# Four more parts of W1 split in the V passes, Q/K's first weights loaded three groups sooner and split one later

## The chip, the cores and the metric

One Trainium2 chip, and of it one core: the program runs on core 0 alone. The metric is the device time of one execution in microseconds (us). A kernel is run several times, and its time is the median.

## The reference, cut to what matters

The input x has 2048 rows of 1024 numbers. Everything starts from one layer norm and ends in one product of two branches:

```python
xn = _layernorm(x)                      # 2048 x 1024
# branch A: attention, 32 heads of 32
qkv = xn @ wqkv                         # wqkv 1024 x 3072
p = softmax(q @ k.T * 32 ** -0.5)
s = (p @ v) @ wo
# branch B: an MLP with the mish activation, 1024 -> 3584 -> 1024
h = xn @ w1 + b1
g = silu((h * tanh(softplus(h))) @ w2)
return x + s * g
```

All inputs are float32. The kernel gets close to float32 products by writing a number as a high part in the format fp32r and a low part (the rest), and adding three products: high by high, high by low and low by high (`THREE`). "Splitting" a weight below means making these two parts: one copy that rounds (the high part) and one subtraction (the low part).

## The kernel before

The program has four stages, one after the other on TensorE (PE).

**Layer norm and V, first pass.** x is read in 16 tiles of 128 rows. A loop over t from 2 to 17 (line 448 on) does one group of V per turn: `v_group(0, t - 2)`, 24 matmuls of 512 columns with the first half of V's weights, and between them the eight transposes of tile t - 1 (`ln_t`). Around that group the turn also does the norm's small steps for later tiles (`ln_a`, `ln_r`, `ln_b`, `ln_x`), the split of the transposed tile (`ln_c`), the load of a later x tile (`x_load`), the store of the group's result (`evac`), from t = 8 on a store of one quarter of a 512-row block of the normed x to DRAM (`xs`, 1 MB), and near the end the loads of the second half of V's weights (`v_load`) and their splits (`v_split`). V's weights of a half come in four pieces of 256 rows; `v_split(i, j, high, rest)` names the engine of the high part and the one of the low part.

**V, second pass.** A loop over t from 0 to 15 with one `v_group(1, t)` per turn and its store `vs`.

**Q and K.** For f from 0 to 15, four groups each (`qk_group`), with the weights of f split by `qk_split(f)` on ScalarE and VectorE. Beside them run jobs (`presplit`) that load half a part of W1 or W2, split it on GpSimd and store it: the parts of W1 that were not split before, then all of W2. From f = 12 on the first head's scores are mixed in (line 558).

**Attention, MLP and the output product**, in an order that a planner (`Plan`) makes from costs written in the program.

What matters around the change is `w1_early`. W1 has 28 parts of 128 columns; the first `W1_V` of them are split during the V passes. Call number f does three things: it stores the finished part f - 2 (`w1s`, 1 MB), loads the raw part f (`w1e`, 0.5 MB in rows of 512 bytes), and lets GpSimd split part f - 1. Its finished parts live in tiles of the tag `w1`, of which there are two, used in turn:

```python
    def w1_tile(name):
        return w1p.tile([P, 2, KT, P], F32R, tag="w1", name=name, bufs=2)
```

`qk_split` takes its tile for Q/K's weights from the same two. So the first Q/K weights, `qkw0`, go into the tile of the last but one part, and their split on ScalarE waits until that part's store has landed in DRAM. The raw parts, the x tiles and V's raw weights share six buffers of the tag `x`.

All loads and stores named here are issued by one engine, SyncE (SP), strictly in the order of the program: an issue that waits for a buffer or for a finished part holds up all that stand behind it. The engines also work in order, each in its own. ScalarE copies each V group's result out of PSUM (`vst`, three buffers) and then makes the high part of the Q/K weights.

In the profile, line 275 is `move` (a DMA between a tile and DRAM of either direction), line 279 is `low` (all low parts, whatever the engine), line 271 is `copy` and line 268 is `act`.

Of the kernel before, what the change touches and what calls it, by code (L numbers as in the profile page):

```python
# [21 lines left out]
NT = S // P  # L22
# [1 line left out]
SCALE = DH ** -0.5  # L24
EPS = 1e-5

W1_V = 16
NS = H * NT
HK = KT // 2

# [183 lines left out]
def body(ctx: ExitStack, tc: tile.TileContext, x, wqkv, wo, w1, b1, w2, out):  # L214
    nc = tc.nc
# [51 lines left out]
    def act(out_, in_, fn, bias=None, scale=1.0):  # L267
        nc.scalar.activation(out_, in_, fn, bias=zero if bias is None else bias, scale=scale)  # L268

    def copy(out_, in_, scale=1.0):  # L270
        nc.scalar.activation(out_, in_, AF.Copy, scale=scale)  # L271

    def move(out_, in_, eng=None):

        (eng or nc.sync).dma_start(out_.bitcast(F32), in_.bitcast(F32))

    def low(eng, out_, in_, high):

        eng.tensor_tensor(out_, in_, high.bitcast(F32), ALU.subtract)  # L279
# [24 lines left out]
    def v_load(i, j):  # L304

        vraw[i, j] = raw = vp.tile([P, 2, 512], F32, tag="x", name=f"vraw{i}_{j}", bufs=XB)
        nc.sync.dma_start(raw, wqkv[j * 256:(j + 1) * 256, 2 * D + i * 512:2 * D + (i + 1) * 512]
                          .rearrange("(k p) f -> p k f", p=P))

    def v_split(i, j, high, rest):  # L310
        raw = vraw.pop((i, j))
        vw[i, j] = w = vp.tile([P, 2, 2, 512], F32R, tag="w", name=f"vw{i}_{j}", bufs=5)
        for k in range(2):
            if high is nc.scalar:
                copy(w[:, 0, k], raw[:, k])
            else:
                high.tensor_copy(w[:, 0, k], raw[:, k])
            low(rest, w[:, 1, k], raw[:, k], w[:, 0, k])

    def v_group(i, t, cut=0, between=None):  # L320
        st = vp.tile([P, 16, DH], F32, tag="vst", name=f"vst{i}_{t}", bufs=3)
        ps = ps1.tile([P, 512], F32, tag="ps", name=f"v{i}_{t}")
        n = 0
        for k in range(KT):
            for a, b in THREE:
                if n == cut and between:
                    between()
                nc.tensor.matmul(ps, xc[t // 4][k // HK][:, a, k % HK, (t % 4) * P:(t % 4 + 1) * P],  # L328
                                 vw[i, k // 2][:, b, k % 2], start=n == 0, stop=n == 3 * KT - 1)
                n += 1  # L330

        def evac():
            copy(st, ps.rearrange("p (h d) -> p h d", d=DH))
            nc.sync.dma_start(vs[i][:, t], st)

        return evac

    def x_load(t):
        xt = vp.tile([P, D], F32, tag="x", name=f"x{t}", bufs=XB)
        nc.sync.dma_start(xt, x[t * P:(t + 1) * P, :])  # L340
        return xt
# [10 lines left out]
    def ln_a(t):  # L352
        xt = xts[t]
        st = vp.tile([P, 2, 6], F32, tag="st", name=f"st{t}", bufs=4)
        mv = vp.tile([P, 2], F32, tag="mv", name=f"mv{t}", bufs=5)
        var = vp.tile([P, 1], F32, tag="var", name=f"var{t}", bufs=5)
        rs = vp.tile([P, 1], F32, tag="rs", name=f"rs{t}", bufs=5)
        for g in range(2):
            nc.vector.bn_stats(st[:, g], xt[:, g * 512:(g + 1) * 512])
        nc.vector.bn_aggr(mv, st)  # L360
        nc.vector.tensor_scalar(var, mv[:, 1:2], EPS, None, op0=ALU.add)
        stat[t] = mv, var, rs

    def ln_r(t):
        mv, var, rs = stat[t]
        act(rs, var, AF.Ln)
        act(rs, rs, AF.Exp, scale=-0.5)

    def ln_b(t):
        mv, var, rs = stat.pop(t)  # L370
        tmps[t] = tmp = vp.tile([P, 1], F32, tag="tmp", name=f"tmp{t}", bufs=3)
        nc.vector.scalar_tensor_tensor(tmp, rs, var, rs, op0=ALU.mult, op1=ALU.mult)
        nc.vector.tensor_scalar(tmp, tmp, -0.5, 1.5, op0=ALU.mult, op1=ALU.add)
        nc.vector.tensor_tensor(rs, rs, tmp, ALU.mult)
        nc.vector.scalar_tensor_tensor(tmp, mv[:, 0:1], -1.0, rs, op0=ALU.mult, op1=ALU.mult)
        tmps[t] = tmp, rs

    def ln_x(t, both=False):
        tmp, rs = tmps.pop(t)
        r = slice(0, D // 2 if both else D)  # L380
        act(xts[t][:, r], xts[t][:, r], AF.Identity, bias=tmp, scale=rs)
        if both:
            r = slice(D // 2, D)
            nc.vector.tensor_scalar(xts[t][:, r], xts[t][:, r], rs, tmp, op0=ALU.mult, op1=ALU.add)

    def ln_t(t):
        xt = xts.pop(t)
        for g in range(2):
            pts_[t, g] = pt = ps1.tile([P, 512], F32, tag="ps", name=f"pt{t}_{g}")
            for k in range(4):  # L390
                nc.tensor.transpose(pt[:, k * P:(k + 1) * P], xt[:, (4 * g + k) * P:(4 * g + k + 1) * P], ident)

    def ln_c(t):
        c, r = t // 4, slice(t % 4 * P, t % 4 * P + P)
        for g in range(2):
            p4 = pts_.pop((t, g)).rearrange("p (k n) -> p k n", k=4)
            copy(xc[c][g][:, 0, :, r], p4)
            low(nc.vector, xc[c][g][:, 1, :, r], p4, xc[c][g][:, 0, :, r])
# [12 lines left out]

    early_w1, w1_steps = {}, iter(range(W1_V + 2))

    def w1_early():
        f = next(w1_steps, None)
        if f is None:
            return
        if f > 1:
            move(w1s[f - 2], early_w1.pop(f - 2)[1])
        if f < W1_V:  # L420
            raw = vp.tile([P, KT, P], F32, tag="x", name=f"w1e{f}", bufs=XB)
            nc.sync.dma_start(raw, w1[:, f * P:(f + 1) * P].rearrange("(k p) f -> p k f", p=P))
            early_w1[f] = [raw, None]
        if 0 < f <= W1_V:
            raw, _ = early_w1[f - 1]
            early_w1[f - 1][1] = w = w1_tile(f"w1p{f - 1}")
            split_w(w, raw, True)
# [12 lines left out]
    v_split(0, 2, nc.scalar, nc.vector)  # L440
    ln_r(1)
    ln_b(1)
    v_split(0, 3, nc.scalar, nc.gpsimd)
    ln_x(1, True)
    ln_a(2)
    ln_r(2)
    xts[3] = x_load(3)
    for t in range(2, NT + 2):
        if t < NT:
            ln_b(t)  # L450
        evac = v_group(0, t - 2, 18 if t == 2 else 8, (lambda: ln_t(t - 1)) if t <= NT else None)
        if t <= NT:
            ln_c(t - 1)
        if t < NT:
            ln_x(t)
        for m in (4, 5, 6) if t == 2 else (t + 4,):
            if m < NT:
                xts[m] = x_load(m)
        if t == 2:
            ln_a(3)  # L460
        if t + 2 < NT:
            ln_a(t + 2)
        if t + 1 < NT:
            ln_r(t + 1)
        if t in (NT - 4, NT - 3):
            for j in range(2):
                v_load(1, 2 * (t - NT + 4) + j)
        if t == NT - 2:
            v_split(1, 0, nc.scalar, nc.vector)
        if t == NT + 1:  # L470
            for j in range(1, 4):
                v_split(1, j, nc.scalar, nc.vector)
        evac()
        if t > 7:
            c, k = t // 4 - 1, t % 4 * 2
            move(xs[c][:, :, k:k + 2], xc[c][k // HK][:, :, k % HK:k % HK + 2])
        if t > NT - 3:
            w1_early()
    for k in (4, 6):
        move(xs[NC - 1][:, :, k:k + 2], xc[NC - 1][1][:, :, k % HK:k % HK + 2])  # L480
# [3 lines left out]
    def qk_load(f):  # L484
        raws[f] = raw_tile(f"qkraw{f}", wqkv[:, (f % 2) * D + f // 2 * P:(f % 2) * D + (f // 2 + 1) * P])
# [7 lines left out]
    for t in range(NT):  # L493
        v_group(1, t)()
        w1_early()
        if t == 9:
            qk_load(0)
        if t == 12:
            qk_split(0)
            qk_load(1)  # L500
    va.close()
# [91 lines left out]
    def load_w1(n):  # L593
# [4 lines left out]
    sp = pool(qb, "sp", 2, side="right")  # L598
    jobs = iter([(1, f, half) for f in range(W1_V, FT) for half in range(2)] +
                [(2, f, half) for f in range(FT) for half in range(2)])  # L600
# [38 lines left out]
    for f in range(2 * KT):  # L639
        for c in range(NC):  # L640
            qk_group(f, c if f < 2 * KT - 1 else (c + 1) % NC)
            presplit()
            if f % 2 and f < 14 and c < 3:
                presplit()
            if c == 0 and f + 1 < 2 * KT:
                qk_split(f + 1)
                if f + 2 < 2 * KT:
                    qk_load(f + 2)
            if f == 8 and c == 0:
                load_head(0)  # L650
            if f == 14 and c == 0:
                load_head(1)
            if f >= 12:
                for kc in range(4):
                    s_mm(0, 4 * (f - 12) + c, kc)
            if f == 2 * KT - 1 and c == 1:
                load_w1(0)
            later.tick()
# [572 lines left out]
    for c in range(NC):  # L1231
        for s in range(4):
            t = 4 * c + s
# [49 lines left out]
```

## Time and profile before

| what | value |
|---|---|
| time, median of 3 runs (lowest to highest) | 3427.58 us (3426.43 to 3434.65) |
| the profiled execution's own time | 3423.3 us |
| its span, first to last instruction | 3421.1 us |
| TensorE busy, share of the span | 3389.4 us, 99% |
| GpSimd busy | 2453.3 us, 72% |
| VectorE busy | 2340.5 us, 68% |
| ScalarE busy | 1942.2 us, 57% |
| mean DMA rate over the span | 155 GB/s |

The table is one execution. The profiled execution is 4.3 us under the median, and 2.2 us of its time lie outside the span. TensorE is busy nearly all the time, so an edit shows in the time only where it changes how long TensorE waits or how fast its clock runs. The other engines' shares are averages over stages that differ much: the DMA engines move 155 GB/s on the whole, but over 300 GB/s in the stages that the change touches.

### The profile page before, as it was taken

Reading aid. Unit: us, or ns where it says so; the run is one execution under the profiler, and the core shown is the slowest. Engines: PE = TensorE matmul, PEld = TensorE weight load, DVE = VectorE, ACT = ScalarE, POOL = GpSimd, SP = SyncE. Lnnn points to the kernel's source line nnn. Section 1 sums busy time; section 2 is a strip of 40 time slices with the busy share of each in tenths; the row PEclk is TensorE's granted clock in tenths of the full one; section 3 lists DMA queues with packets and bytes.
Section 4 is the critical chain, followed back from the end, with each engine's and each line's share of the span. In section 5 each row is a group of like instructions: output and inputs, shape, how many; then the busy total and the mean of one; then the engine's idle time right before and its main releaser. Section 6 shows DMA issues by size and latency. Waiting matters only on the chain.

```text
span 3421.1 us, 45658 instructions
## 1 busy us (share of the span) xinstructions
PE 3389.4 (99%) x17059; PEld 2492.7 (73%) x17059; DVE 2340.5 (68%) x3763; ACT 1942.2 (57%) x3086; POOL 2453.3 (72%) x752
## 2 busy tenths in 40 slices
PE   8999999999999999999999999999999999999999
PEld 7878877677777767777677777777777767777687
DVE  6211226877878777788878787878878788776533
ACT  5211112766666667666666676666666666666621
POOL 0444443988888888888888888888888888888700
PEclk9999999999999999999999999999999999999999
DMA  5989888433334354343434443333445443333482
GB/s 200 326 292 317 301 309 289 124 109 102 118 106 124 102 170 132 116 112 111 124 99 124 149 148 111 112 113 110 124 112 183 123 123 112 112 114 121 136 297 85
DMA packets 289184, 529.60 MB, mean 155 GB/s; under 512 B 88426, under 2 KB 134506, under 8 KB 265706
## 3 DMA queue, kind: packets, MB, share of 16 engines
q1 hardware_dynamic: 269108, 484.74, 46.0%
q10 hardware_dynamic: 19856, 41.95, 3.3%
q8 instruction: 135, 2.21, 0.3%
q14 instruction: 85, 0.70, 0.1%
HBM read 386.89 MB, written 138.67 MB: 154 GB/s over the span
## 4 chain that ended last, share of the span: by engine, by line
PE 87%; DMA 7%; POOL 3%; DVE 2%; SPq 1%; ACT 0%; issue 0%; POOLq 0%; ACTq 0%; DVEq 0%
PE y L1027 18%; PE h L938 17%; PE t L790 13%; PE pv L837 13%; PE s L707 13%; PE op L1124 5%; DMA w2s<-pw 3%; PE v L328 3%; PE qk L631 3%; DMA w1s<-pw 2%; POOL pw L279 1%; DMA w1e<-in_B_w_dram 1%; PE zp L863 1%; DVE mx L713 1%; POOL pw L619 1%; POOL w1p L279 0%
## 5 line engine op out<-in xcount | busy, mean ns | idle before, releaser
L819 POOL TENSOR_TENSOR z<-z,p 128x2048 f32<-128x2048 f32 x448 | 2066.5, 4613 | 192.1 <-ACT p L268 162.5
L268 ACT ACTIVATE p<-t,zero 128x512 f32<-128x512 f32 x2048 | 1384.4, 690 | 636.1 <-PE t L790 618.3
L713 DVE TENSOR_REDUCE mx<-s 128x1 f32<-128x512 f32 x1984 | 1329.6, 686 | 435.4 <-PE s L707 427.8
L1027 PE MATMUL y<-w,act 128*128 128x512 f32 x2688 | 937.4, 391 | 0.6 <-DVE yacc L1047 0.5
L790 PE MATMUL t<-qstack,kstack 128*128 128x512 f32 x2048 | 801.5, 393 | 0.3 <-ACT p L268 0.2
L707 PE MATMUL s<-kstack,qstack 128*128 128x512 f32 x1984 | 779.6, 394 | 3.9 <-DVE mx L713 3.4
L938 PE MATMUL h<-xr,w 128*128 128x512 f32 x2016 | 713.5, 391 | 2.1 <-DMA w<-w1s 2.1
L1027 PEld LDWEIGHTS y<-w,act 128*128 128x128 f32 x2688 | 502.9, 188 | 118.4 <-issue 8.4
L790 PEld LDWEIGHTS t<-qstack,kstack 128*128 128x128 f32 x2048 | 384.0, 188 | 109.0 <-issue 16.8
L707 PEld LDWEIGHTS s<-kstack,qstack 128*128 128x128 f32 x1984 | 371.3, 188 | 126.5 <-issue 24.3
L837 PE MATMUL pv<-p,v 128*32 128x512 f32 x4096 | 459.4, 594 | 0.0
L938 PEld LDWEIGHTS h<-xr,w 128*128 128x128 f32 x2016 | 377.7, 188 | 85.1 <-issue 5.0
L631 PE MATMUL qk<-xc,qkw 128*128 128x512 f32 x1536 | 352.6, 390 | 6.1 <-ACT qkw L271 6.0
L631 PEld LDWEIGHTS qk<-xc,qkw 128*128 128x128 f32 x1536 | 288.9, 188 | 67.3 <-ACT qkw L271 6.4
L837 PEld LDWEIGHTS pv<-p,v 128*32 128x32 f32 x4096 | 123.3, 110 | 282.7 <-issue 282.0
L819 POOL TENSOR_TENSOR z<-p,p 128x2048 f32<-128x2048 f32 x32 | 147.9, 4623 | 243.3 <-ACT p L268 162.3
L1047 DVE TENSOR_TENSOR yacc<-yacc,y 128x512 f32<-128x512 f32 x416 | 283.0, 680 | 52.2 <-PE y L1027 51.4
L938 PE MATMUL h<-xc,w 128*128 128x512 f32 x672 | 242.3, 391 | 0.1
L279 DVE TENSOR_TENSOR qst<-qk,qst 128x512 fp32r<-128x512 f32 x64 | 44.2, 691 | 253.6 <-ACT qst L271 253.6
L271 ACT ACTIVATE qst<-qk 128x512 fp32r<-128x512 f32 x64 | 38.3, 598 | 308.6 <-PE qk L631 235.5
L619 POOL CAST pw<-praw 128x512 fp32r<-128x512 f32 x80 | 50.9, 637 | 195.7 <-DMA w2s<-pw 125.2
L328 PE MATMUL v<-vw,xc 128*128 128x512 f32 x768 | 181.1, 395 | 0.2 <-DVE xc L279 0.2
(93 smaller groups left out, 2366.5 us busy)
## 6 DMA issues: line engine op xcount, KB each, us to landing
w<-w1s SPq DMA_DIRECT2D x112, 1024.0 KB
w<-w2s SPq DMA_DIRECT2D x224, 512.0 KB
w2s<-pw SPq DMA_DIRECT2D x56, 512.0 KB
qstack<-qs SPq DMA_DIRECT2D x96, 256.0 KB
kstack<-ks SPq DMA_DIRECT2D x96, 256.0 KB
praw<-in_B_w_dram SPq DMA_DIRECT2D x80, 256.0 KB
x<-in_A_x_dram SPq DMA_DIRECT2D x32, 512.0 KB
w1s<-w1p SPq DMA_DIRECT2D x16, 1024.0 KB
```

Source lines behind the costliest of these rows:

```text
L268: nc.scalar.activation(out_, in_, fn, bias=zero if bias is None else bias, scale=scale)
L328: nc.tensor.matmul(ps, xc[t // 4][k // HK][:, a, k % HK, (t % 4) * P:(t % 4 + 1) * P], vw[i, k // 2][:, b, k % 2], start=n == 0, stop=n == ...
L631: nc.tensor.matmul(ps, w[:, a, k], xc[c][k // HK][:, b, k % HK], start=n == 0, stop=n == 3 * KT - 1)
L707: nc.tensor.matmul(sp_, qst[h % 3][:, qt * P:(qt + 1) * P], kst[h % 3][:, kc * 512:(kc + 1) * 512], start=True, stop=True)
L713: nc.vector.reduce_max(tiles["mx"][:, qt, kc:kc + 1], tiles[qt, kc], axis=AX.X)
L790: nc.tensor.matmul(tp, kst[h % 3][:, kt * P:(kt + 1) * P], qst[h % 3][:, c * 512:(c + 1) * 512], start=True, stop=True)
L819: nc.gpsimd.tensor_tensor(zs[h], pts[T - 1] if kt == 1 else zs[h], pts[T], ALU.add)
L837: nc.tensor.matmul(pv[h][c * DH:(c + 1) * DH, :], vt[h][:, k, :], pts[T - kt + k][:, c * 512:(c + 1) * 512], start=k == 0, stop=k == NT - 1)
L938: nc.tensor.matmul(t["h"], w1t[n][:, a, k], xts_[c][k // HK][:, b, k % HK], start=i == 0, stop=i == 3 * KT - 1)
L1027: nc.tensor.matmul(t["y"], acts[n][:, p, s * P:(s + 1) * P], w2t[m_][:, q], start=j == 0 and i == 0, stop=j == YB - 1 and i == 2)
L1047: nc.vector.tensor_tensor(ya, ya, t["y"], ALU.add)
L1124: nc.tensor.matmul(ps[t, dh], ohl[t // 4, k][:, a, s * P:(s + 1) * P], wt[k][:, b, r], start=k == 0 and i == 0, stop=k == KT - 1 and i == 2)
```

## The change

There are four edits, all in the V passes and at the start of Q/K.

1. `W1_V` is 20 instead of 16, and `w1_early` is called from t = 10 of the first pass on instead of from t = 14. Each call f therefore comes four groups sooner than before, and there are four calls more; the last one (it stores the last part) is in turn 13 of the second pass in both kernels. The jobs of Q/K lose parts 16 to 19 of W1, which is eight jobs of 80, and the number of slots for jobs falls from 85 to 78.
2. x tiles are loaded three turns ahead instead of four.
3. `qk_load(0)` is issued in turn 6 of the second pass instead of turn 9, and `qk_split(0)` stands in turn 13 instead of turn 12. As part numbers moved too, `qkw0` now takes the tile of part 18; before it took the tile of part 14.
4. The fourth piece of V's first weights gets its low part from VectorE instead of GpSimd, and its split stands behind the norm of tile 1 instead of ahead of it.

```diff
-W1_V = 16
+W1_V = 20
...
-    v_split(0, 3, nc.scalar, nc.gpsimd)
     ln_x(1, True)
+    v_split(0, 3, nc.scalar, nc.vector)
     ln_a(2)
     ln_r(2)
     xts[3] = x_load(3)
...
-        for m in (4, 5, 6) if t == 2 else (t + 4,):
+        for m in (4, 5) if t == 2 else (t + 3,):
             if m < NT:
                 xts[m] = x_load(m)
...
-        if t > NT - 3:
+        if t > NT - 7:
             w1_early()
...
     for t in range(NT):
         v_group(1, t)()
         w1_early()
-        if t == 9:
+        if t == 6:
             qk_load(0)
-        if t == 12:
+        if t == 13:
             qk_split(0)
             qk_load(1)
...
             qk_group(f, c if f < 2 * KT - 1 else (c + 1) % NC)
             presplit()
-            if f % 2 and f < 14 and c < 3:
+            if f % 2 and f < 14 and c in (0, 2):
                 presplit()
```

## The prediction

> **What bounds the kernel now.** I read the page first, for which engine sets the time.
>
> ```profile
> PE 3389.4 (99%) x17059; PEld 2492.7 (73%) x17059; DVE 2340.5 (68%) x3763; ACT 1942.2 (57%) x3086; POOL 2453.3 (72%) x752
> ```
>
> TensorE is busy in 3389.4 of 3421.1 us, so at most 31.7 us can be won by filling its gaps, and any edit costs or gains what it adds to or takes from them. The second view is the list of waits, TensorE's alone:
>
> ```profile
> core 0 of [0], span 3421.1 us
> engine line waited for: us in total, times, longest us
> PE pt L391 <- ACT x L268: 11.9, 2, 9.4
> PE qk L631 <- ACT qkw L271: 6.0, 1, 6.0
> PE s L707 <- DVE mx L713: 3.4, 5, 1.9
> PE h L938 <- DMA w<-w1s: 2.1, 1, 2.1
> PE s L558 <- DVE mx L562: 1.5, 1, 1.5
> ```
>
> Five entries hold 24.9 us. The change touches three: the norm's start (pt), Q/K's first weights (qk), and the first scores (L558), which lie in Q/K. I went to the second one with the timeline from 176 to 236 us, because it is the place that edits 1 and 3 move:
>
> ```profile
> 188.21 1.73 SPq L288 DMA_DIRECT2D qkraw<-in_A_wqkv_dram  x1
> ...
> 204.93 1.26 POOL L279 TENSOR_TENSOR w1p<-w1e,w1p 128x512 fp32r<-128x512 f32 x1
> 206.22 0.32 SPq L275 DMA_DIRECT2D w1s<-w1p  x1
> ...
> 210.11 1.15 ACT L271 ACTIVATE qkw<-qkraw 128x512 fp32r<-128x512 f32 x2 [19.73 <-DMA w1s<-w1p]
> 210.78 1.29 DVE L279 TENSOR_TENSOR qkw<-qkraw,qkw 128x512 fp32r<-128x512 f32 x2 [89.56 <-ACT qkw L271]
> ...
> 210.80 25.42 PE L631 MATMUL qk<-xc,qkw 128*128 128x512 f32 x105 [5.95 <-ACT qkw L271]
> ```
>
> The first Q/K matmul comes at 210.80, after 5.95 us in which TensorE had nothing to do: V's last one ended at 204.85. The raw Q/K weights were issued at 188.21 and are not what is late: ScalarE's copy at 210.11 was released by the landing of a store, w1s from w1p. This is the tile wait: `qkw0` takes the tile of part 14, and that tile is free when part 14 is stored. The chain back is: GpSimd ends part 14's split at 204.93 + 1.26 = 206.19, SP issues the store at 206.22, and it lands just ahead of 210.11. So what ends last at this point is the stream of W1's parts through DMA and GpSimd. The windows say what limits that stream:
>
> ```profile
> core 0: us, PE busy (x) PEld busy (x) DVE busy (x) ACT busy (x) POOL busy (x), PEclk, DMA share, GB/s
> 76.00:102.00 26.00, 26.00 (x136) 21.95 (x135) 13.52 (x38) 14.23 (x27) 0.00 (x0) 1.00 0.85 290
> 94.00:100.30 6.30, 6.30 (x34) 5.29 (x33) 2.70 (x5) 4.32 (x8) 0.00 (x0) 1.00 0.54 161
> 102.00:137.00 35.00, 35.00 (x162) 29.09 (x161) 9.30 (x10) 10.31 (x17) 16.25 (x16) 1.00 1.01 339
> 125.00:135.00 10.00, 10.00 (x46) 8.29 (x45) 0.00 (x0) 1.20 (x2) 6.04 (x7) 1.00 1.05 394
> 137.00:206.50 69.50, 67.84 (x300) 55.84 (x298) 0.00 (x0) 5.99 (x10) 41.14 (x44) 1.00 1.00 329
> 205.00:211.00 6.00, 0.20 (x1) 0.21 (x2) 0.23 (x1) 0.89 (x2) 4.99 (x6) 0.65 0.50 198
> 211.00:213.00 2.00, 2.00 (x5) 1.57 (x6) 1.51 (x3) 1.72 (x4) 1.69 (x1) 0.50 0.00 0
> 213.00:215.00 2.00, 2.00 (x9) 1.55 (x9) 1.51 (x2) 0.00 (x0) 0.00 (x0) 0.84 0.69 161
> ```
>
> Before the clock column stand the engines' busy times; the last three columns are the granted clock, the share of the 16 DMA engines that is busy, and GB/s. From 102 to 206.5 us the DMA engines are busy all the time (1.01 and 1.00), at 339 and then 329 GB/s. TensorE is full up to 204.85, and the DMA is full as well: two bounds run side by side there, and the DMA one finishes later.
>
> **The change part by part.**
>
> *Edits 1 and 3, the parts of W1 and Q/K's first weights.* The sizes, in the answer on DMAs for 150 to 180 us:
>
> ```profile
> w1s<-w1p SPq DMA_DIRECT2D x5, 1024.0 KB
> w1e<-in_B_w_dram SPq DMA_DIRECT2D x5, 512.0 KB
> ```
>
> Before, `qkw0` waits for the store of part 14, ahead of which stand 15 stores and 16 loads of parts. After, it takes the tile of part 18: 19 stores and 20 loads stand ahead. V's stores ahead of it are the same in both, those up to turn 12. So 4 x (1024 + 512) KB = 6.29 MB are added to what must have passed SP's queue before the first Q/K weight can be split. At the 329 GB/s of the long window that is 19.1 us.
>
> What comes in return is an earlier start: the first call moves from about 102 to about 76 us. But the DMA isn't idle there. In 76 to 102 its share is 0.85, so 0.15 x 26 = 3.9 us are free. The four parts thus need 19.1 us, and 3.9 us are there: the store of the last part that matters lands 19.1 - 3.9 = 15.2 us later. Loading Q/K's raw weights three turns sooner doesn't help, as they weren't late, and they only move ahead of three V stores in the same queue. Splitting one turn later than before cancels nothing either: that call of `w1_early` stores part 19, behind the store that `qkw0` waits for. So the gap before Q/K grows from 5.95 to about 21.2 us. **Cost: +15.2 us.** Low end: the four parts at the best rate of the table, 394 GB/s, 16.0 - 3.9 = 12.1. High end: the free 3.9 can't be used, 19.1. I take the middle value, since it rests on the long window in which this very stream runs.
>
> Behind that wait on ScalarE stand the evacuations of V's last two groups; they only feed stores, and who waits for them is PSUM banks, of which there are eight. On SP, part 19's store and the next raw Q/K weights stand behind; the second Q/K weights are needed four groups after the first, and move with them. The clock: during a gap of 5.95 us it falls to 0.50 in the row from 211 and is at 0.84 in the one after. That loss is 2 x 0.50 + 2 x 0.16 = 1.3 us, it is in the time of before, and a longer gap pays it once as well. **0 us.**
>
> *Edit 4 and the start.* The rows of before, from the timeline of the first 32 us (start, time, engine, line):
>
> ```profile
> 16.11 1.14 ACT L271 ACTIVATE vw<-vraw 128x512 fp32r<-128x512 f32 x2
> 16.68 0.21 DVE L372 SCALAR_TENSOR_TENSOR tmp<-rs,var 128x1 f32<-128x1 f32 x1
> 16.80 2.50 POOL L279 TENSOR_TENSOR vw<-vraw,vw 128x512 fp32r<-128x512 f32 x2 [7.19 <-ACT vw L271]
> 16.93 0.15 DVE L373 TENSOR_SCALAR tmp<-tmp 128x1 f32<-128x1 f32 x1
> 17.12 0.99 DVE L374 TENSOR_TENSOR rs<-rs,tmp 128x1 f32<-128x1 f32 x1
> 18.14 1.18 DVE L375 SCALAR_TENSOR_TENSOR tmp<-mv,rs 128x1 f32<-128x1 f32 x1
> 19.36 0.81 ACT L268 ACTIVATE x<-x,tmp,rs 128x512 f32<-128x512 f32 x1 [2.11 <-DVE tmp L375]
> 19.36 0.55 DVE L384 TENSOR_SCALAR x<-x,rs,tmp 128x512 f32<-128x512 f32 x1
> 19.82 1.28 DVE L359 BATCH_NORM_STATS2 st<-x 128x6 f32<-128x512 f32 x2
> ...
> 22.66 0.16 DVE L374 TENSOR_TENSOR rs<-rs,tmp 128x1 f32<-128x1 f32 x1
> ```
>
> GpSimd's two subtractions from 16.80 to 19.30 stand beside two tiny VectorE steps that take 0.99 and 1.18 us, where the same step takes 0.16 at 22.66. So about 1.85 us are lost ahead of tile 1's norm at 19.36. With the subtractions gone from GpSimd, that norm starts at about 17.5. Then ScalarE needs 0.81 for it and 1.14 for the high parts of the fourth piece, to 19.5, and VectorE, which does the two low parts (1.29 a pair of this shape in the row at 210.78), is through at about 20.2 instead of free at 19.82 for the statistics of tile 2. The copies of tile 1 into xc stand behind a step on ScalarE that needs those statistics (`ln_r(2)` ahead of `ln_c(1)`), and TensorE needs them next. They come some 0.35 us later, not sooner: what was won goes to the new work in front. The Trainium skill, "SBUF — State Buffer", section "Who interferes with whom", says that a VectorE instruction with two SBUF inputs and a GpSimd instruction that reads SBUF block each other for the whole instruction; the rows 17.12 and 18.14 agree. By that rule alone edit 4 would gain the 1.85, and the moved parts of edit 1, whose GpSimd work now stands beside the norm's small steps in turns 11 to 17, would pay some of it back; I give both nothing in the sum, for the reason that follows.
>
> TensorE's part of the V passes then ends 0.35 us later, but it has 21 us to wait for the weights. So this is covered. **0 us** (-1.85 to +0.35 if the cover were gone).
>
> *Edit 2*, x one turn later. A tile is then issued one turn ahead of its statistics instead of two. A late one would hold VectorE, and through it TensorE in a later turn; the list of waits of before has no wait of TensorE that a load of x ended, and the same 21 us cover what comes of it. **0 us.**
>
> *Eight jobs fewer in Q/K.* Here TensorE is the bound, and the jobs lie beside it:
>
> ```profile
> 300.00:480.00 180.00, 180.00 (x796) 149.05 (x795) 35.21 (x49) 27.80 (x49) 81.59 (x85) 1.00 0.91 310
> ```
>
> It is busy 180 of 180 us with the DMA share at 0.91. Eight jobs of 256 KB in and 512 KB out take load off, but there is nothing to win where TensorE has no gap. The only gap is the 1.5 us at the first scores (L558 above), which depends on when VectorE gets through the weights of f = 13. It may shrink: 0 to -1.5, I take **-1.0 us**.
>
> **Sum.** 15.2 + 0 + 0 + 0 - 1.0 = +14.2 us. On the profiled execution's 3423.3 us that is 3437.5. The median before, 3427.58, is 4.3 above that execution; the forecast for the median is 3427.58 + 14.2 = 3441.8, rounded **3442 us**, or +0.41%.
>
> **The rivals.**
>
> *The queue speeds up and the gap closes (not slower).* The rate isn't fixed: between 125 and 135 us it was 394 GB/s, with a deep queue. With four parts more in flight from 76 us on, the queue is deep all along. The bytes: 339 x 35 + 329 x 69.5 = 34.7 MB passed from 102 to 206.5; with the four parts 41.0. At 394 the stretch from 76 takes in 26 x (394 - 290) = 2.7 MB beforehand, and 38.3 MB need 97.2 us instead of 104.5. Q/K's weights would be ready before 204.85; the 5.95 and the 1.3 of the clock would go: -7.3 - 1.0 = -8.3, 3419.3 us. It decides from 372 GB/s on, where (41.0 - 26 x 0.082) / 0.372 = 104.5. Against it: in 137 to 206.5 the share is 1.00 at 329 GB/s, so the packets themselves take this time, and the mix (a third of a part's bytes comes in 512-byte rows) stays. Chance 0.10. The Trainium skill, "DMA: Bandwidth & Descriptors", section "Where 436 GB/s comes from", names about 358 GB/s as the limit between HBM and SBUF for a core; held to it, the stream would still be (41.0 - 1.8) / 0.358 - 104.5 = 5 us late. The 394 of the 10 us row lies above that limit, so the measurement stands and the chance stays.
>
> *It speeds up by half.* At 355 GB/s: (41.0 - 1.7) / 0.355 = 110.7, that is +6.2, and +5.2 with the jobs: 3432.8 us. The same rows speak for and against. Chance 0.15.
>
> *SP gets stuck sooner, and a hole opens (worse).* In the changed program's order the last raw piece of V's second weights takes the buffer of the first, so its issue waits until VectorE has split that one in turn 14. Behind it on SP stand a V store, a quarter of xs, part 1's store and part 3's load. Before, such a wait stood at the same place, and the share fell to 0.54 in 94 to 100.3. If the free 3.9 us are not filled and the hole of 6.3 x 0.46 = 2.9 us comes on top: 19.1 + 2.9 - 1.0 = +21.0, 3448.6 us. For it: part 1's store can't leave sooner than that. Against it: enough is queued ahead by then. Chance 0.10.
>
> **How the numbers follow.** The forecast has 0.65. About 0.3%, 10.3 us, is what a measurement of this kernel can tell from no change. Of the forecast's own range, 12.1 - 1.5 = +10.6 to 19.1 - 0 = +19.1, nearly all is above that: 0.60 of its 0.65 slower, 0.05 within. The half case is 0.12 within and 0.03 slower, the worse case 0.10 slower, the closed gap 0.06 within and 0.04 faster. Together slower 0.73, same 0.23, faster 0.04. The range: the half case's middle is +5.2 and the worse case's +21.0; from 3431 (a little under the half case) to 3450 (a little over the worse one) leaves out the closed gap and some tails.
>
> **What would show it.** Right: TensorE's wait for qkw at line 631 at 18 to 24 us, still released by the landing of a w1s store; the DMA share near 1 from 80 us to the start of Q/K; the first Q/K matmul near 226; from there on the same distances as before. Wrong: that wait gone or under 6 us, with V passes moving over 370 GB/s; or TensorE waiting inside the V passes, which would mean x or V's weights came late; or a Q/K stage whose length differs by more than 2 us, which I call bound by TensorE.

## The result, and the profile after

| | before | after |
|---|---|---|
| time, median (lowest to highest), taken in turn on one chip | 3429.43 us (3423.57 to 3434.65), 7 runs | 3440.01 us (3435.78 to 3440.98), 7 runs |
| the profiled execution: time, span | 3423.3, 3421.1 | 3435.78, 3433.9 |

The ratio is 1.0027, with a 95% interval of 1.0015 to 1.0038: the changed kernel is slower by 10.6 us in the medians and by 12.8 us between the two profiled spans. The forecast was +14.2 us, 3442 us; 3440.01 lies in the range.

The page's first row, busy time by engine:

```profile
PE 3391.2 (99%) x17059; PEld 2493.8 (73%) x17059; DVE 2344.3 (68%) x3765; ACT 1943.4 (57%) x3086; POOL 2449.5 (71%) x750
```

TensorE is busy 1.8 us longer in a span that is 12.8 longer: the loss is idle time. The first row of TensorE's list of waits in the changed kernel (columns: engine, tile and line that wait, what ended the wait, then us in total, times, longest):

```profile
PE qk L631 <- ACT qkw L271: 18.7, 1, 18.7
```

The wait for Q/K's first weights has gone from 6.0 to 18.7, inside the 18 to 24 that were forecast. The two waits at L558 (1.5 in the list before, and another of 0.4 below what was quoted) are gone from the list. The timeline of the changed kernel around that wait (start, length, engine and line):

```profile
195.88 0.32 SPq L275 DMA_DIRECT2D w1s<-w1p  x1
...
217.78 1.26 POOL L279 TENSOR_TENSOR w1p<-w1e,w1p 128x512 fp32r<-128x512 f32 x1
219.06 0.32 SPq L275 DMA_DIRECT2D w1s<-w1p  x1
224.43 1.15 ACT L271 ACTIVATE qkw<-qkraw 128x512 fp32r<-128x512 f32 x2 [12.86 <-DMA w1s<-w1p]
225.11 2.50 PE L631 MATMUL qk<-xc,qkw 128*128 128x512 f32 x5 [18.65 <-ACT qkw L271]
```

The store at 219.06 is part 18's (part 19's, the last of 20, follows at 225.18), and with three more stores left out between them the one at 195.88 is part 14's. The chain is the one told before, four parts further on: GpSimd ends part 18's split at 219.04, SP issues its store at 219.06, it lands, ScalarE copies at 224.43, TensorE starts at 225.11. The windows (the last three numbers of a row are the granted clock, the DMA share and GB/s):

```profile
76.00:102.00 26.00, 26.00 (x132) 21.87 (x131) 14.13 (x37) 14.73 (x27) 7.52 (x8) 1.00 0.98 339
102.00:137.00 35.00, 35.00 (x164) 29.12 (x163) 8.24 (x13) 9.77 (x16) 15.80 (x16) 1.00 1.05 396
137.00:206.50 69.50, 69.46 (x307) 57.19 (x305) 0.00 (x0) 6.59 (x11) 39.90 (x43) 1.00 0.97 317
206.50:225.00 18.50, 0.00 (x0) 0.00 (x0) 0.00 (x0) 1.17 (x3) 12.18 (x14) 0.62 0.96 322
```

The DMA engines are full from 76 us to Q/K, as forecast. What was not forecast is the rate in 102 to 137: 396 GB/s against 339 before.

Part of this is one small transfer that changed its place. The load of `b1` (line 481, 14 KB) brings 3584 single numbers of 4 bytes, and it stands on SP behind the last stores of xs. Before, it ran from 134 to 137 us, a stretch with 3584 packets under 512 bytes; in the changed kernel it ran from 146.5 to 150. These stretches as windows, in the kernel before and then in the changed one:

```profile
134.00:137.00 3.00, 3.00 (x15) 2.49 (x14) 0.00 (x0) 0.60 (x1) 0.57 (x1) 1.00 0.92 100
```

```profile
146.50:150.00 3.50, 3.50 (x17) 2.92 (x16) 0.00 (x0) 0.00 (x0) 2.36 (x3) 1.00 0.73 74
```

The DMA engines are busy there for most of the time and move 100 and 74 GB/s. Without the load of b1 the stretch from 102 us on has 361 GB/s before and 396 after, and the one up to 206.5 has 330 in both (after: (317 x 69.5 - 74 x 3.5) / 66 = 330). So 22 of the 57 GB/s by which the first of them became faster, and the whole fall of the second from 329 to 317, are b1's load, which went from the one window into the other.

The whole difference, cut at three events of the two profiled executions (end of V's last matmul; first matmul at L631; the pair of matmuls at L535 that closes the Q/K stage). That last event in the timeline of the kernel before, and then of the changed one:

```profile
578.67 0.33 PE L535 MATMUL mtp<-ident_r,hl 128*128 128x128 f32 x2
```

```profile
589.48 0.33 PE L535 MATMUL mtp<-ident_r,hl 128*128 128x128 f32 x2
```

| stretch | before | after | after - before |
|---|---|---|---|
| start to V's end | 204.85 | 206.46 | +1.61 |
| wait for Q/K's first weights | 5.95 | 18.65 | +12.70 |
| Q/K stage | 367.87 | 364.37 | -3.50 |
| all after it | 2842.43 | 2844.42 | +1.99 |
| span | 3421.1 | 3433.9 | +12.8 |

The first two rows go together: the weights come when the queue brings them, so the first Q/K matmul is 14.31 us later whatever V's end does. The last row is no effect of the change: over all kernels run here this stretch takes 2842.4 to 2844.4, with 20 parts as with 16. That leaves +14.3 - 3.5 = +10.8, which is what the medians show (+10.6).

### The profile page after: what moved, and what is told of

Read it like the earlier page. It is cut to its first block, busy times and chain, and to the rows that moved or that the text cites. A ratio compares the mean times of both kernels' runs of the same rounds, so it can differ in the third digit from the quotient of the medians.

```text
span 3433.9 us, 45655 instructions
## 1 busy us (share of the span) xinstructions
PE 3391.2 (99%) x17059; PEld 2493.8 (73%) x17059; DVE 2344.3 (68%) x3765; ACT 1943.4 (57%) x3086; POOL 2449.5 (71%) x750
## 4 chain that ended last, share of the span: by engine, by line
PE 95%; DVE 2%; DMA 2%; POOL 1%; SPq 1%; ACT 1%; issue 0%; ACTq 0%; POOLq 0%; DVEq 0%
PE y L1027 18%; PE h L938 17%; PE t L790 13%; PE s L707 13%; PE pv L837 13%; PE qk L631 10%; PE op L1124 5%; PE v L328 3%; DMA w1e<-in_B_w_dram 1%; PE zp L863 1%; DVE mx L713 1%; POOL w1p L279 0%; PE pt L391 0%; PE s L558 0%; SPq L275 0%; SPq L334 0%
## 5 line engine op out<-in xcount | busy, mean ns | idle before, releaser
L631 PE MATMUL qk<-xc,qkw 128*128 128x512 f32 x1536 | 352.4, 390 | 18.7 <-ACT qkw L271 18.7
L631 PEld LDWEIGHTS qk<-xc,qkw 128*128 128x128 f32 x1536 | 289.2, 188 | 79.3 <-ACT qkw L271 19.1
```

The lines of the kernel that those rows point to most:

```text
L631: nc.tensor.matmul(ps, w[:, a, k], xc[c][k // HK][:, b, k % HK], start=n == 0, stop=n == 3 * KT - 1)
```

## The experiments

### The number of parts: 16 and 18 with the earlier start

**e1**: the changed kernel with 16 parts, and with them the places for jobs of before.

```diff
-W1_V = 20
+W1_V = 16
-            if f % 2 and f < 14 and c in (0, 2):
+            if f % 2 and f < 14 and c < 3:
```

> The changed kernel with only the number of early parts put back (16, and the slots for the jobs with it); the earlier start, the x loads, the places of the Q/K load and split and the fourth piece stay changed. Queue theory (the bytes ahead of the tile that Q/K's first weights take, at the rate of the DMA): four parts of 1536 KB at 329 GB/s are 19.1 us fewer, so the first Q/K matmul comes at 225.1 - 19.1 = 206.0 at the earliest, that is right after V's last one (206.5): a wait of 0 to 1 us in place of 18.65, no fall of the clock, and 18 to 20 us less than the changed kernel, about 3421 on the median, 7 to 9 under the kernel before. Rival (the place of the split, one turn later, or the load, is what made it late): the wait stays above 10 us.

**e2**: 18 parts, nothing else changed.

> The changed kernel with 18 early parts instead of 20 (76 jobs in 78 slots). Queue theory: two parts fewer ahead, 2 x 1573 KB at 329 GB/s = 9.6 us, first Q/K matmul at 215.5, wait 9.1 us, and 9 to 10 us less than the changed kernel. Loop theory (a part costs a turn of the loop load, split, store, at 5.6 us whatever the bytes): 2 x 5.6 = 11.2, first matmul at 213.9, wait 7.4. Rival (the place of the split): 18 us.

The experiments ran on three chips, so a kernel is compared by its ratio to the kernel before on its own chip. The kernel before took 3429.43 us beside the changed kernel, 3426.01 beside e1 to e4, 3425.78 beside e5 to e8, and 3425.61 (one run) beside e9 to e11.

| parts | first Q/K matmul | wait | time (runs) | ratio to before, 95% |
|---|---|---|---|---|
| 16 (e1) | 207.80 | 2.68 | 3420.08 (11) | 0.9986, 0.9977 to 0.9995 |
| 18 (e2) | 212.19 | 7.00 | 3424.00 (10) | 0.9997, 0.9988 to 1.0006 |
| 20 (changed kernel) | 225.11 | 18.65 | 3440.01 (7) | 1.0027, 1.0015 to 1.0038 |

So the number of parts makes the loss: with 16 the earlier start is a gain. From 18 to 20 parts the first matmul moves by 12.9 us, 6.5 a part. In e2 it came sooner than either theory had it (215.5 and 213.9). These are single executions, and they differ: in e7 below, whose V passes are those of the changed kernel, the first Q/K matmul comes at 223.37 instead of 225.11. By the ratios e1 is 0.41% or 14 us faster than the changed kernel, where 18 to 20 were expected, and its forecast of no wait failed by 2.7 us. The timeline of e1 shows why:

```profile
201.96 0.32 SPq L275 DMA_DIRECT2D w1s<-w1p  x1
202.38 5.20 SPq L334 DMA_DIRECT2D vs<-vst  x4
206.63 0.60 ACT L271 ACTIVATE vst<-v 128x512 f32<-128x512 f32 x1 [4.35 <-DMA vs<-vst]
207.12 1.14 ACT L271 ACTIVATE qkw<-qkraw 128x512 fp32r<-128x512 f32 x2
207.80 10.54 PE L631 MATMUL qk<-xc,qkw 128*128 128x512 f32 x44 [2.68 <-ACT qkw L271]
```

The copy at 207.12 is not released by a store of W1. It starts when ScalarE is done with the evacuation of a V group at 206.63, and that one waited 4.35 us for its buffer, whose store of V stands on SP behind part 15's store at 201.96. Here it is the order on ScalarE that ends last.

### The order on ScalarE, tested: Q/K's first split one turn sooner

**e6** is e1 with the split moved back to where it stood before.

```diff
-        if t == 13:
+        if t == 12:
             qk_split(0)
```

> 16 parts and the 85 places for jobs again, as in e1, and Q/K's first split one turn sooner (t == 12). In e1 2.7 us of waiting were left although the store of part 14 had landed some 7 us earlier; ScalarE's copy stood behind the evacuation of V's group 13, which waited for its buffer. If that order on ScalarE is the whole of the 2.7 us, the wait for qkw at L631 goes, the first Q/K matmul comes at 205.1 to 205.6 and the time is 2.7 us (and up to 1 us of clock) under e1's: 3416 to 3418. The rival: the store still ends last (with part 15 not yet split at t == 12), the evacuation of group 12 then waits on ScalarE for it and 1 to 3 us of wait remain at the banks of V or at qkw: 3419 to 3421.

The same stretch of the timeline in e6:

```profile
202.22 1.14 ACT L271 ACTIVATE qkw<-qkraw 128x512 fp32r<-128x512 f32 x2
...
204.93 13.31 PE L631 MATMUL qk<-xc,qkw 128*128 128x512 f32 x58
```

The weights are split from 202.22 on, and Q/K follows V with no gap. 3418.3 us (11 runs, 3413.18 to 3421.33), ratio 0.998 (0.9971 to 0.9989): 1.6 us more gained on the kernel before than in e1 (7.5 against 5.9), where 2.7 were expected. The clock's part is seen here too: from the first Q/K matmul to the first score at L558 it takes 266.56 us in e6 (471.49 - 204.93), 268.02 in the kernel before (478.82 - 210.80) and 268.12 in the changed kernel (493.23 - 225.11). So its gap costs the kernel before 1.5 us of granted clock (the prediction had 1.3), and the changed kernel's, three times as long, 1.6. Over the other kernels with a gap of 4.5 us or more it is 2.1 to 3.0, with a granted clock of 0.50 in the first 4 to 6 us behind the gap; behind the gaps of 2.7 and 3.1 us in e1 and e9 the clock stays at 1.00 and the difference is 0.4.

### What the earlier start is worth by itself

**e10**: 20 parts as in the changed kernel, but the first call where it was before; the four calls left out come as second calls in four turns of the second pass.

```diff
-        if t > NT - 7:
+        if t > NT - 3:
             w1_early()
...
         w1_early()
+        if t in (1, 4, 7, 10):
+            w1_early()
```

> The changed kernel with 20 parts, but the first part started where the kernel before starts it (t > NT - 3); the four calls that this leaves out come as second calls in turns 1, 4, 7 and 10 of V's second pass. It measures the earlier start by itself. By the prediction's term the earlier start is worth 3.9 us (the free share of the DMA engines between 76 and 102 us): first Q/K matmul near 229. By the stores of part 14 (issued at 206.22 before, at 195.88 in the changed kernel) it is worth 10.3 us: 234 to 236. If doubled calls keep the queue deeper and make the loop faster, it lies under 229.

The timeline of e10 ahead of Q/K, and then its windows:

```profile
205.53 0.32 SPq L275 DMA_DIRECT2D w1s<-w1p  x1
...
233.11 1.15 ACT L271 ACTIVATE qkw<-qkraw 128x512 fp32r<-128x512 f32 x2 [18.67 <-DMA w1s<-w1p]
233.79 2.50 PE L633 MATMUL qk<-xc,qkw 128*128 128x512 f32 x5 [27.57 <-ACT qkw L271]
```

```profile
76.00:102.00 26.00, 26.00 (x132) 21.86 (x131) 13.28 (x37) 14.49 (x27) 0.00 (x0) 1.00 0.84 291
102.00:137.00 35.00, 35.00 (x164) 29.14 (x163) 9.53 (x12) 10.35 (x17) 16.26 (x16) 1.00 1.03 356
137.00:206.50 69.50, 69.22 (x306) 57.00 (x304) 0.00 (x0) 5.38 (x9) 41.21 (x44) 1.00 0.96 308
206.50:225.00 18.50, 0.00 (x0) 0.00 (x0) 0.00 (x0) 1.19 (x2) 11.90 (x14) 0.61 1.04 344
```

(L633 is the changed kernel's L631; the edit adds two lines.) Part 14's store is issued at 205.53, close to the 206.22 of the kernel before, and the first matmul comes at 233.79: the earlier start is worth 233.79 - 225.11 = 8.7 us, or 10.4 against the 223.37 of e7. The 233.79 is a little under the 234 to 236 that the stores had suggested, and the 8.7 is more than twice the 3.9 of the prediction. The time of e10 is 3444.05 us (one run). From the kernel before to e10, with the start the same, four parts cost 233.79 - 210.80 = 23.0 us, where the prediction had 19.1. The windows say where the rest of the start's gain lies: 76 to 102 moves 291 GB/s here and 339 in the changed kernel (48 x 26 = 1.2 MB, at 329 GB/s 3.8 us, which is the 3.9 that was forecast), but 102 to 137 moves 356 and 396 (40 x 35 = 1.4 MB, 4.3 us more) and 137 to 206.5 moves 308 and 317 (0.6 MB, 1.9 us more). From 206.5 to 225 e10 makes up 1.2 us (344 against 322), which leaves 8.8. How the gain splits between the two middle windows hangs on b1's load, which lies across their border in e10; their sum doesn't.

### What limits the stream in the last 70 us: GpSimd in the loop, or the DMA

**e4**: from the ninth part on the low halves are made by VectorE, which is idle there (0.00 in the window from 137), instead of GpSimd.

```diff
-            split_w(w, raw, True)
+            split_w(w, raw, True, nc.vector if f > 8 else None)
```

> The changed kernel, but VectorE, idle in V's second pass, makes the low half of each W1 part split there; GpSimd keeps the high halves. Bytes and their order stay. Queue theory (the DMA engines are full): the first Q/K matmul stays at 225 within 2 us and the rate within 137 to 206.5 stays near 317 GB/s. Loop theory (load, split of 3.8 us on GpSimd, store, in two tiles): the split takes about 2 us instead of 3.8, some 1.8 us a part over 11 parts, so the first Q/K matmul comes up to 20 us sooner, the wait falls under 5 us, and the rate in that window rises to about 390 GB/s.

The window of e4:

```profile
137.00:206.50 69.50, 68.42 (x302) 56.31 (x300) 16.68 (x20) 7.17 (x12) 18.66 (x27) 1.00 1.02 343
```

First Q/K matmul at 217.93 after a wait of 12.52; 3431.14 us (10 runs, 3428.1 to 3432.18), ratio 1.0015 (1.0006 to 1.0024). It falls between the two theories: 7.2 us are won (5.4 against e7's 223.37), so GpSimd's time was part of the loop, and 12.5 are left, with the share now at 1.02. **e9** asks which of the two is left, with 18 parts and the same edit.

> 18 parts as in e2, and from the ninth part on the low halves are made by VectorE instead of GpSimd, as in e4. In e2 the first Q/K matmul came at 212.19 after a wait of 7.0 us; in e4, with 20 parts, moving the low halves brought it from 225.1 to 217.9. Theory 'DMA is the limit once GpSimd is out of the way': two parts fewer than e4 at e4's 343 GB/s (1572.9 KB each, 4.6 us) put it at 208.8, a wait of 3 to 4 us. Theory 'the loop of two tiles alone': e2's 212.2 less e4's gain of 7.2 is 205.0, V's end, and the wait is under 1 us.

The first matmul came at 209.87 after 3.07 us (one run, 3419.02). The theory that the DMA is the limit once GpSimd is out of the way had 208.8 and 3 to 4 us; the loop alone had 205.0 and under 1. What the loop is made of stands in the changed kernel's waits of GpSimd and of SP from 137 to 225 us:

```profile
POOL w1p L406 <- DMA w1e<-in_B_w_dram: 37.1, 14, 8.8
```

```profile
SPq L275 <- POOL w1p L279: 35.8, 11, 5.1
```

All waits of GpSimd end with the landing of a raw part, none with a tile that comes free. SP issues the next raw part only behind the store of a finished one, and for these it waits 35.8 us for GpSimd. So it is not the two tiles that close the loop but SP's order: split, store, next load, split. With both halves of the split on GpSimd that stream runs at 317 GB/s, with the low half on VectorE at 343 (b1's load lies in both windows). That the DMA engines are what is left then fits e9's number, but is not shown: in e4 SP still waits 30.3 us for the low halves, and a share of 1.02 is no proof of the best rate.

### The start: the edit or the clock

V's end moved by 1.61 in the changed kernel, and edit 4 was put at 0.35 there. **e3** is the changed kernel without edit 4, **e5** the kernel before with edit 4 alone.

```diff
-    ln_x(1, True)
-    v_split(0, 3, nc.scalar, nc.vector)
+    v_split(0, 3, nc.scalar, nc.gpsimd)
+    ln_x(1, True)
```

> The changed kernel with edit 4 undone: GpSimd makes the fourth piece's low part again, ahead of tile 1's norm. Cover theory: V's last matmul ends at 204.9 instead of 206.5, but the first Q/K matmul stays at 225.1 within 1 us, so its wait grows to about 20.2 and the span doesn't change. Rival (the start counts): the first Q/K matmul comes 1.6 us sooner, and the span is 1.6 us shorter. The clock in 23 to 26 us goes back to 1.00.

> The kernel before with edit 4 alone. If edit 4 lengthens the start by itself (theory 'edit', from the 1.6 us by which V's end moved in the changed kernel), V's last matmul ends near 206.4. If the 1.6 us was the granted clock of that one execution (theory 'clock', from the granted clock of 0.89 between 11 and 27 us there and 1.00 in the three runs in which V ended near 205.2), it ends at 205.1 to 205.4 with a granted clock of 1.00 in 11 to 27, or near 206 with 0.89. The first Q/K matmul stays where the queue puts it, 210.8, in both; a time within 0.1% of before.

| kernel | edit 4 | granted clock in 11 to 27 us | V's last matmul ends |
|---|---|---|---|
| before | no | 1.00 | 204.85 |
| e3 | no | 0.89 | 205.82 |
| changed kernel | yes | 0.89 | 206.46 |
| e1 | yes | 1.00 | 205.12 |
| e5 | yes | 0.93 | 206.71 |
| e2 | yes | 1.00 | 205.19 |
| e4 | yes | 1.00 | 205.41 |
| e6 | yes | 1.00 | 204.93 |
| e11 (e6's kernel once more) | yes | 0.92 | 206.66 |

(First Q/K matmul less the wait; in e6 and e11 there is no wait.) The first 27 us as one window, in e11 and then in e6 (the clock is the third number from the end):

```profile
11.00:27.00 16.00, 12.77 (x47) 8.77 (x46) 13.62 (x33) 8.84 (x19) 0.00 (x0) 0.92 0.39 132
```

```profile
11.00:27.00 16.00, 11.95 (x54) 8.38 (x53) 13.73 (x33) 8.83 (x19) 0.00 (x0) 1.00 0.36 128
```

With a full clock V ends 0.1 to 0.6 us later with the edit than in the kernel before; with 0.89 to 0.93 all ends lie 1 to 1.9 us later, with the edit and without, and the kernel of e6 and e11, twice the same, differs by 1.73. So the granted clock of a single execution is enough for the 1.6. e5 alone doesn't decide it: its 206.71 lies near the 206.4 of the one theory, and near the 206 that the other has for a low clock. In e3 the first Q/K matmul comes at 224.01, 1.1 us sooner than in the changed kernel and 0.6 later than in e7, which has the edit; the clock there, expected to go back to 1.00 in 23 to 26 us, was 0.90. In e5 it comes at 211.19, where 210.8 was expected. The time of e3 (3435.38) is 1.0027 of the kernel before on its chip, as the changed kernel's is, and e5 (3425.47) differs from the kernel before by 0.3 us (one run each).

### The jobs: their number or their places

The Q/K stage became 3.5 us shorter, and all of it after the first score. **e7** puts the dense places back into the changed kernel, with its 72 jobs; **e8** spreads the 85 places of e6, with its 80 jobs, evenly.

```diff
-            if f % 2 and f < 14 and c in (0, 2):
+            if f % 2 and f < 14 and c < 3:
```

> The changed kernel with the 85 places for jobs of before (c < 3), 72 jobs as in the changed kernel. Theory 'places': the 3.6 us by which Q/K's part behind the first scores became shorter come from the thinner places (6 instead of 7 in each pair of turns); with the dense ones back the wait of s at L558 returns (1 to 3 us) and the stage from the first Q/K matmul to the move at L535 is 367 to 368 us long: 3442 to 3444. Theory 'number': with 72 jobs the last ones are through before f = 13's weights anyway, the waits at L558 stay away and the stage has 364 to 365 us: 3439 to 3441.

```diff
-            if f % 2 and f < 14 and c < 3:
+            if f < 14 and c in ((0, 2) if f % 2 else (1,)):
```

> e6 with the 85 places spread evenly: two extra in an odd f, one in an even f, where e6 has three extra in the odd ones. 80 jobs as before. Theory 'places': the waits at L558 go as in the changed kernel, the Q/K stage is 364 to 365 us long instead of 367.9, and the time is 2.5 to 3.6 us under e6's: 3413 to 3415. Theory 'number': the waits stay near 1.7 and 0.7 us and the time is e6's, within 0.5 us.

In TensorE's list of waits for e7 the ones at L558 are back; the list of e8 has none:

```profile
PE s L558 <- DVE mx L562: 2.1, 1, 2.1
...
PE s L558 <- DVE qst L279: 1.2, 2, 0.7
```

The time of e8 is 3414.89 us (5 runs, 3412.87 to 3415.29), ratio 0.9968 (0.9955 to 0.998): 10.9 us under the kernel before on the same chip (3425.78), and by the ratios (0.9968 and 1.0027) some 20 under the changed kernel. It beats both. e7 is at 3438.42 (4 runs), under what either theory had, but beside it the kernel before is 3.65 us faster than beside the changed kernel. Its ratio is 1.0039 (1.0025 to 1.0053) against 1.0027 (1.0015 to 1.0038): 4 us slower, as the places would have it, though the intervals overlap and its first weights came 1.7 us sooner. The whole Q/K stage was longer than expected in e7 (370.4 us, against 367 to 368) and shorter in e8 (362.8, against 364 to 365); the clock behind the gap ahead of it plays into both. Behind the first score the clock is full, and there the kernels fall into two groups:

| kernel | jobs, places in an odd f and the even f before it | from the first score (L558) to L535 |
|---|---|---|
| before, e1, e5 | 80, 7 and 4 | 99.85, 101.17, 100.76 |
| e7 | 72, 7 and 4 | 101.53 |
| changed kernel, e3, e4, e10 | 72, 6 and 4 | 96.25 each |
| e2, e9 | 76, 6 and 4 | 96.25 each |
| e8 | 80, 6 and 5 | 96.25 |
| e6 | 80, 7 and 4 | 96.36 |

So it is the places, not the number. e6 is the exception: it has the dense places and no wait at L558 in its profiled execution, whose 3413.18 was far under its ten others (3416.89 to 3421.33). **e11** is the same kernel once more.

> e6's kernel a second time, since its profiled execution (3413.18) was 4 to 8 us under its ten others (3416.89 to 3421.33) and showed no wait at L558. If the dense places bring that wait in some executions and not in others, a typical execution (near 3418) shows 1 to 3 us of waits of s at L558 and 366 to 368 us from the first Q/K matmul to the move at L535, against 362.9 in the first profile. If the time is near 3418 without these waits, the spread comes from elsewhere.

At 3419.26 it showed waits of 1.7 and 0.3 at L558, 366.8 us for the stage, and 100.2 from the first score on. The dense places bring the wait in most executions, and the even ones in none of those profiled. What ScalarE waits for from 440 to 600 us, in e11 and in e8:

```profile
ACT qst L271 <- DMA w2s<-pw: 22.5, 4, 7.8
ACT qst L271 <- DMA praw<-in_B_w_dram: 12.5, 2, 7.4
ACT qst L271 <- DMA ks<-qst: 11.8, 2, 6.0
```

```profile
ACT qst L271 <- DMA w2s<-pw: 7.1, 1, 7.1
ACT qst L271 <- DMA ks<-qst: 3.4, 1, 3.4
```

The copy of a Q/K result out of PSUM waits for DMA landings 46.8 us in e11 and 10.5 in e8 (58.1 in the kernel before, 22.0 in the changed one, and 33.1 in e6, where it did not reach TensorE). It needs a free `qst` buffer, and that is free when an earlier Q or K store has landed. The names w2s and praw are those of the landings that came last by the profile; that these transfers of the jobs, which SP issues, delay the Q and K stores, which ScalarE issues, is the likely reading, but it was not tried by itself.

## Why the prediction was right or wrong

**The bound and the chain: right.** The wait that grew is the one named, 18.7 in 18 to 24, released by a store of W1; first Q/K matmul at 225.11 against "near 226"; DMA share 0.96 to 1.05 from 76 us on. e1 and e2 show that the parts make it, and e3 that edit 4 does not.

**Term 1, four parts at 329 GB/s, 19.1 us: too small.** With the start unchanged they cost 23.0 (e10). In the changed kernel itself parts 14 to 18 take from 195.88 to 219.06, 5.8 us a part. The step that failed is "at the 329 GB/s of the long window": the rate of that window is not a constant. With four parts more, e10 moves 308 in it, 21 x 69.5 = 1.5 MB less, or 4.4 us; its 356 in 102 to 137 gives 0.6 MB or 1.8 us back, and 19.1 + 4.4 - 1.8 = 21.7 leaves 1.3 of the 23.0, which I can't assign (b1's load lies in both sums). In the last stretch SP issues a raw part only behind GpSimd's split of an earlier one, and e4 won 7.2 us there by taking half of GpSimd's work away.

**Term 2, the earlier start, 3.9 us: too small by more than half.** It is 8.7 (e10; 10.4 by e7). The free share in 76 to 102 was filled as forecast, from 0.85 to 0.98. But the prediction took a share of 1.00 to mean that nothing more fits. In 102 to 137 the share went from 1.01 to 1.05 only, and the rate from 339 to 396: a busy DMA engine is not one at its best rate. 22 of these 57 GB/s are b1's load, which left that window. The other 35 came while SP's issues waited 10.5 us of the 35 for other engines, against 20.0 before; that the deeper queue made them is argued, not shown. This is the mechanism of the first rival, which did come true, in that stretch alone: the rate passed 370 GB/s, and the gap still did not close, because the last 70 us did not go faster (330 GB/s outside of b1's load, as before). The Trainium skill, "DMA: Bandwidth & Descriptors", section "Where 436 GB/s comes from", which the prediction weighed, holds transfers between HBM and SBUF to about 358 GB/s; the row of 396 GB/s over 35 us does not agree. "HBM Reference", section "Specifications (TRN2)", says that a core streaming alone gets well above that, some 425; the row agrees with that sentence.

**Their sum: right, by two errors that cancel.** 23.0 - 8.7 = 14.3 measured, 19.1 - 3.9 = 15.2 forecast. That the sum came out was luck: one term is 3.9 us too small and the other 4.8. The whole change was forecast at +14.2 and is +10.6 in the medians; most of what lies between is the jobs' term below. The 3440.01 lies nearer to the forecast 3442 than that, because the kernel before took 3429.43 in the comparison and not the 3427.58 that the forecast started from.

**Edit 4: right.** The timeline of the changed kernel shows each of its steps:

```profile
17.18 0.16 DVE L374 TENSOR_TENSOR rs<-rs,tmp 128x1 f32<-128x1 f32 x1
17.37 0.16 DVE L375 SCALAR_TENSOR_TENSOR tmp<-mv,rs 128x1 f32<-128x1 f32 x1
17.57 0.81 ACT L268 ACTIVATE x<-x,tmp,rs 128x512 f32<-128x512 f32 x1 [1.30 <-DVE tmp L375]
...
20.14 1.28 DVE L359 BATCH_NORM_STATS2 st<-x 128x6 f32<-128x512 f32 x2
```

The two small steps take 0.16 each with GpSimd's subtractions gone (0.99 and 1.18 before), the norm starts at 17.57 (forecast 17.5), and the statistics of tile 2 at 20.14 instead of 19.82, 0.32 later (forecast 0.35). The price was covered by the wait, as said. The Trainium skill's "SBUF — State Buffer", section "Who interferes with whom", agrees with these two rows. What it would pay back beside the moved parts shows in one step: beside a subtraction of GpSimd from 94.36 to 95.65 the step of line 372, 0.21 in most turns, takes 1.04:

```profile
94.36 1.29 POOL L279 TENSOR_TENSOR w1p<-w1e,w1p 128x512 fp32r<-128x512 f32 x1
...
94.62 1.04 DVE L372 SCALAR_TENSOR_TENSOR tmp<-rs,var 128x1 f32<-128x1 f32 x1
```

In e10, where GpSimd does nothing there, the same step takes 0.21 at 94.10. This 0.83 was covered too.

**Edit 2: right.** No wait of TensorE is ended by a load of x (one held VectorE for 0.18 us), and V ends at 204.93 to 205.41 where the clock was full (e1, e2, e4, e6).

**Eight jobs fewer, -1.0 with a floor of -1.5: wrong.** It is -3.5, outside its bounds. The step that failed is the bound: "the only gap is the 1.5 us at the first scores". Equal turns would have told. In the kernel before, a turn of 4 score and 24 Q/K matmuls starts every 6.35 us, but two take longer (the rows of line 558 in its timeline):

```profile
485.16 0.85 PE L558 MATMUL s<-kstack,qstack 128*128 128x512 f32 x3
487.49 0.50 PE L558 MATMUL s<-kstack,qstack 128*128 128x512 f32 x1 [1.47 <-DVE mx L562]
493.66 1.07 PE L558 MATMUL s<-kstack,qstack 128*128 128x512 f32 x4
500.01 1.07 PE L558 MATMUL s<-kstack,qstack 128*128 128x512 f32 x4
506.36 0.61 PE L558 MATMUL s<-kstack,qstack 128*128 128x512 f32 x2
507.39 1.10 PE L558 MATMUL s<-kstack,qstack 128*128 128x512 f32 x2 [0.42 <-DVE qst L279]
514.16 1.07 PE L558 MATMUL s<-kstack,qstack 128*128 128x512 f32 x4
```

From 485.16 to 493.66 are 8.50 and from 506.36 to 514.16 are 7.80: 2.15 + 1.45 = 3.6 lost, where the list counts 1.47 + 0.42. Nor was the prediction right that it hangs on how many jobs there are (e7, e8). It named a Q/K stage that differs by more than 2 us as a sign against it, and that sign came.

**The rival with a hole on SP** did not come: 94 to 100.3, where the share was 0.54, is full in the changed kernel's window:

```profile
94.00:100.30 6.30, 6.30 (x34) 5.29 (x33) 3.35 (x9) 3.63 (x7) 1.57 (x2) 1.00 1.04 417
```

## What to carry to other kernels

Moving work into a stretch where the compute engine is full but the DMA is full too only moves the end of the queue: ask which store the next stage waits for, and count the parts ahead of it; here four parts fewer with the earlier start turn a loss of 10.6 us into a gain of 5.9 (e1), and with Q/K's first split one turn sooner into one of 7.5 (e6). Take no share of 1.00 for a fixed rate, look for small transfers of single numbers in a window before its rate is carried over, and measure a loss on the bounding engine by the pitch of equal turns, since the list of waits can show half of it. Side jobs that share the DMA engines with the main loop want even places: e8 does the same jobs as e6 in better places, and is 3.4 us faster and spreads less (2.4 us over 5 runs, against 8.2 over 11).

## What the runs showed of the hardware that was not expected

The 16 DMA engines of this core moved 396 GB/s over 35 us, and 417 over 6.3 us, at shares of 1.05 and 1.04; in the same stretch of the kernel before they were nearly as busy (1.01) at 339. A load of 14 KB in 3584 single numbers took 3 to 3.5 us of them, at 100 and 74 GB/s and shares of 0.92 and 0.73. In the first 27 us the granted clock was 1.00 in some executions and 0.89 to 0.93 in others, even of one and the same kernel (e6, e11), and without a cause that these runs show; it moves V's end by 1 to 1.9 us, which a comparison of two single profiles takes for an effect of the edit.
